# Another issue table for a fused attention and gate kernel: 272 runs of value blocks instead of 356

## The chip, the cores and the metric

The kernel runs on one core of one Trainium2 chip. The metric is the device time of one execution in microseconds (us). Times before come from three runs and from one profiled execution, whose trace gives the start and length of every instruction.

## What is computed

```python
def reference(A_x, A_wqkv, A_wo, B_x, B_w1, B_w3, B_w2):
    x = A_x                                   # [1, 2048, 512]; B_x is not used
    xn = layernorm(x)
    # A: attention, 32 heads of 16
    qkv = (xn @ wqkv).reshape(B, S, 3, 32, 16).transpose(2, 0, 3, 1, 4)
    q, k, v = qkv
    p = softmax(einsum("bhqd,bhkd->bhqk", q, k) * 16 ** -0.5)
    s = einsum("bhqk,bhkd->bhqd", p, v).transpose(0, 2, 1, 3).reshape(B, S, 512) @ wo
    # B: gated feed-forward, 1792 wide, on the same xn
    h = silu(xn @ w1) * (xn @ w3)
    g = silu(h @ w2)
    return x + s * g
```

All of it is float32.

## The kernel before

A prologue (up to about 159 us) normalizes the tokens, makes queries, keys and values, and stores queries and keys in DRAM. A main part then does the attention and the gate together, and a short end finishes the output.

**Products in float32.** Matrix products are done as three products of a high and a low half of each operand (names end in h and l: xth, xtl, wh, wl). In the attention the three stand below each other in one contraction: a head's 16 rows appear as 3 x 16 rows of queries and keys.

**Two row halves.** Scores, maxima and gate products contract over 64 rows or fewer, so TensorE's array is used as two halves of 64 rows, lower and upper, that can run one matmul each at the same time. Value products contract over 128 keys and use the whole array.

**The letters.** The main part's order of matmuls is written out in the string `ORDER_OF_ISSUE`, one letter per piece of work. A small letter stands for the lower half of the array, a capital for the upper one:

- `s`, `S`: a score matmul (line 627, tile e), 128 keys by 512 queries of one head of a pair; ScalarE then takes the exponential into a tile pt (line 630).
- `m`, `M`: a matmul for the row maximum of a later phase (line 389, tile m); VectorE reduces it into mp (line 391). A phase is one pair of heads and half of the queries: 32 phases, 16 key chunks each.
- `f`, `F`: one matmul of the gate (line 858, tile f). A product's lower and upper matmuls add up in one bank; ScalarE takes the bank out, GpSimd (POOL) does the rest and splits weights and hidden rows.
- `v`: a value block (line 640, tile pv): the four exponentials of a chunk times the values, 8 instructions in the trace. It needs the whole array.
- `r`, `R`: the small work that turns a phase's maxima into rows of the query tile, a transpose on TensorE among it; `r` is followed by a value block.
- `o`: a piece of the output projection or of the division by the sums, on the whole array.

There are 7 PSUM banks for s, m, f and o together, and one for pv. A **stretch** below is what stands between two pieces of work on the whole array; a **run** is such pieces in a row.

**The planner.** As the program is built, the letters are read one after the other. The class `Model` is an account of time: `half` books a matmul of one half, `whole` one of the whole array, `work` the engine that empties a bank. `SLOT` (0.232) is the time of a half's matmul, `LOAD` (0.1) its weight load, `TURN` (0.097), `VALUES` (0.858) and `CLEAR` (0.983) belong to value blocks. By this account the planner chooses the bank that comes free first, and places DMAs, small work and gate elements that are due. A letter whose work isn't ready by the account goes to a list `late` and is tried again before each next letter:

```python
    for c in ORDER_OF_ISSUE:
        settle()
        small()
        tend()
        catch_up()
        ...
            what = (c.lower(), int(c.isupper()))
            if what in late or not half_issued(*what):
                late.append(what)
```

Nothing of this runs on the chip; the chip sees fixed queues of instructions with semaphores.

Of the kernel before, what the change touches and what calls it, by code (L numbers as in the profile page):

```python
# [55 lines left out]
    "FMfFffFMsFfmFSfMfFfsMfFFfSfMfSfmFvmSMmmFmFvvvsMfSfFSffMfFFsfMFsfFsMFfFsmFSffFmSFffSrvsMfMfSFffFsFmFf"
    "SFmsFfFfMsFFmFsFmFfSmvmSfSMsMfvmSMmMsvvfMfSSfMfSffMfSfFfMfFsFmFsFsFmFfFsFmFsFfMfFfSmMfSfsMffSsvmSSff"
    "MsMvsSmSmMvvSfMffSfMfSfSfMfMfFfFmFsFfFfFsMfFfSmSfFfFmFsFmFmFsFfFsFfFmSfFmFsFfFfMfMfMsMvsMfMMsvsMSmFm"
    "vSmmFFmmFmFmFvvvmSmFfFFmsFFfmFsFFfsFfMSfFfMfSfMfMfSfFffMsFFfSfMfSfFfMfsFsRvvSmMffSfSfMffSfSmFfFsFmFs"
    "FFfMfFsFfsMFffSMffSfFmSfFsFMfFfSfmFsFsFmFFfmFsFSffFmMvSmsSmMvsFmSmSmFvvmFSmsMsFvsMFmMssFvsMMmsSvsFmS"  # L60
    "FmmSvSmfFmSfSfFFfmSfFmFsFFffSmFsFfFMsfFSfMffFFsmMvsMMmmFmFvvvsMfSfFMfFffSmSfFmFsFfFMfSfMfFfsMfFFssFr"
    "vvSmfFSfFmfSFfmSfFsFMfsFFfmFSffFMsfFFsMffSFfMffMMfsFFfFfMsfFFmFsFfMfmFsFFfMfmFFfMsvvSmsSSmvmSsMvvMff"
    "SSffFMfFssFmFfFsFMfsFFfMfSfmFsFFffFfMSffMSffSfMfFsFfMsFfFmFsFsFmFfFsFmFmFfSmvmSmSSfvmSmMMsvSmSmvSmSf"
    "FfMffFSfmSFfMfsFfFmFsFFfMfsFmFFmFfMfmMvvvMsMsfFfFFsfFMsfFsFFfmFFssFFfMfSffSsFrvvSfMffSfMSffSfMfMfFfS"
    "fFsFmFfFsFmFsFmFsFfFsMfSfFmMvSmmSmFFsvSmmSMsvMsMfsFsFfFFfMsfFFsmFSffFMsFffMfFMfSfMsvmSMmfSvvMfSsfFmF"
    "FfFsmFFfsFMfSffSmFFffSMfFfSfMmvSmFmmFsFvSmmSMsvSmmFfSSffFfFmSfFsFMfFsfFMsfFFsMffSFfMmvSmFmMmvvSfMffM"
    "fSfSfSfMfFfFsFmFsFfFmSfFsMfFfFmFsFmFmMvvrsMFfsFMfFsFfMsFfsFMfSfFfmSfFmFsFmFfFMfMfmSvvSfMfMffSfSfMfSf"
    "FfMfFsMfFsFfMfFsFfMsFsFfFmFsFfMmFfMfSvSmsMMsvSmmSfMvsMMmSffSvvMffSfMfSfMfSfSfFfFmFsFmFsFfSfMfFsFmSFf"
    "FmSfFsFmFfFsMfMfFsMfFsFFsFfFfMfSfMssFvSmMmFsvSmFsmFmSvSmmMsSvSmFsFsmMvSmmFmFsFFmmFmFvvvMsfSMffSfFfFs"
    "MfFFsMffSFffMsFfSMffMFfSfFfSfsMFfFffSSfsSRvvvsMfMMfSffFFffMsFfFFsfMsFfFMfsFmFSfmFFfSffSfFmFmFsFFmFfs"  # L70
    "FmFFfSffMFfsMvvSmSsMmvSmMmfSvvMfmSFmFsfFfFsFmFFfsFsFmFsFFfmFsFFfMsFfsFMfFsFfmMfFSfSfFmvvSmmSfSFfFfFf"
    "mFfSfMfSFffMsFmFfFsFmFMfmFFfMsvvsMfSsFFmFffFMsFfSfmFFsFfsMFfmFfSFfFsmMvSmmSSfvMssSmMvMsSfMfSmvmSMmSs"
    "vvmSfSSfMfFffFSfMffSSfmFFfsFmFFfFsmFsFfMsFmFsRvvSmFfMfSffMFfMfSffFmFmFsFFfFsMfFffFsFFmMmvsMFmsSvMssS"
    "mMvvmFFssFsMFfFfMffSfFMsfFSfMfsFfFmSFffFfSmSvMmsFfFfFfSFmfSfFSmfFfSmFSffFmSfFmFSfmFfFmMvSmMssFvmSsMM"
    "svmSmFsFfSfFFmsFFfmFSfmFfSFmfFMsFfmMvvsMMssMvMsMsfSMfvvMfSffMMfMffSfMfSffFfFsFmFfFsFsFFmFsFffMsFFfMm"
    "RvSmSfSffMfFfFmSfFfSmFsFfFMsfFmFsFMffFsFSfMmvsMMmmFvvSfmFfSSfmFfFSfmFsFFfmSFfFsmFFsFfMmFffMSfvsMfSMs"
    "vvMfSsFfFmFsfFsFmFfFsFsFMffFmFSffFMfmMvvSfMffSfMSffSfMfSfFfFmFsFmFsFfFsFmFfFsMsFfMmFvsMfSfMmSvSmfSsF"
    "FmfFfFsMFffSmFSfFfMsfFmFsFmFfFMfMfMmvvfSMmMmvvsMFmFsFfFsFfmFsFfFsFMfSfMfSffFfMsFsFMfRvMsfMSffSfSfMSf"
    "vMsMfSfSsvmSSfmMvMsSfSfMsvmSfSFfFmFfFsmFFsmFFfsFFmsFFmFfSffMfMSfFffSMfSffFSfmFsFFfmSfFsFMfMffFmMvsMf"
    "MmMvvmMsMFsFsvsMSmSmvsMFsfFSmFffFmFSfmFfSFffMsFFmfFsMFfSffFFmSfFsMfMfFfsFMffFsFfFMfsSvMfSssMMfvsMmMS"  # L80
    "svSmFmmSvSmmFmMmFvvvmSfFsFmFFsfFSmFfsFFmFsfFSmfFmFmFsFFfsFFmFffMSfMfSffMSfRvsMfMfSMfSffMfSfMfSvSmfMs"
    "FsFFfFfMsFfsFmFFsfFmSfFMfmFsFFfsMvSmmSFfFfsFFfmFSfsFmFmFvvvvmSfFFfsSMffFFfFsmFFsfSfMFfFsFmFmfFmSvSmM"
    "mfMSfvSmSfMsvMsMfsFFfFsFfMsFfsFmFfSfFmSfFfSFmfFmFsSvmSSfMfsMvsMmMMmvvvfSMffSfMSffSFfmFsFFfmSfFsFfFMf"
    "SfsFsFmFFfsFrvMsfMfSfFfSFffMfSFmFsMfFfSfmFfFsFmFFfsFmFmMvsMFfsFFmFsFfsFMfSfSfmFFffSmFSffFmFFmMfvSmMs"
    "SfMfvsMMsSsvmFSmSmvvMffSfMfFsMFffSfMFfsFSfmFSfFfmFfFsFFmFffSMfsFfFFmfFSfmFsFfSmFFfmFSfFmfFSfmFmMvvsM"
    "sMsMvsMMfMsvSfMsFmFsFfFfmFFsFmfFSmFfSfMfFfsFMfMfMfFfMmvvvsMSffSfFfFmFsFfFsFmFFsFffSMfFfSfSmFfSfsFrvv"
    "SmfSfFFfSmfFSmFfSffFSmfFSffMsFFfMfsFmFFmFffMsFfFmFFsfFfSmFfSfFFmsFmFfMFsFfmMvmSfSSmvMsMsMsvsMfMMfSsv"
    "sMMsMsvvMffMSfMffSfFsFfFmFsFmFmFSffFmFsFFfmFMffSvsMSsSmvMfMsfFFssFFfmFFsFfsFmFSffSmFfFfSMffMfFSmvmSM"
    "fsMvSmsSFmmFvSmmSMmvvmSSfSfmFfFFfMsfFFsMfsFfFMsfFMffSsFfFMffMfSSffSfMrMsMsvSmmMsSvvSfMffSSffMfMfMfSf"
    "MfsFfFfFFsFmFsFmsFFfMfsFfMfFMsfFFmSfFffMsFmFFfSfmFfFSfmFfFmSvvSmsSmFFmvSmSmMmvvmFsFMfmFsFFfFsFmFfSff"  # L90
    "MFssFfFMfSffMfSfFfSmFfFsFMsFfFsMfFffMFffSfMSmvvsMmMsMvvSfMfSffMfMfSfMfFsFfFsMfFsFfFsMfFmFsFsFfFmFfSf"
    "MmFfSfSfFmFfSfFmFsFmFfSmFfMmvvMsSssFvrvSmfSSfmFfFfFmSFfFsmFFsFfmFsFsFsFmFfFFfmSFfmFsFFfmFSsfFmMvvSmS"
    "sMmvsMMsSfvmSMsSsvmFSfMfFfsMFfFsmFFfSfmFFfSffMfFsFmFfFMmfMvvMffMfSfSfSfFMffFsFFfMsFfFsmFfFFsmSfFFmmF"
    "vsMMmSfvsMsFFfMfFsFfmSFfSfmFFsfFmSFfmFSfSffFMfmFMmvvSsMsmMvvsMfMfSFffSfMSffMfSfMfFsFsFfMFfsFmFsFmFmF"
    "FmFmFsvvsMfFFmsFfFFmMfsFfFfSFfMsFfSfMfFfSfMfFsMRvvsMMffSSffFFfMsFfSfMfsFfFmFsFFmsFFfmFFmfSmSvSmmSSmv"
    "SmMfsSvMssMSmvsMsFFmFfFfSmSfFfMfSfFmSfFfFmSfmFFsmFfFMmvvMsfSMfsMvMsmSsSvMsFmsFsFfFfFmFSffSmFFsFfMfsF"
    "fFMfmFMffSvsMmSsMvsMfMSfSmvsMfMfMsFfFFfSfmFfFSmfFfSfMFfSffMmFmFvvvvRFsFmFfMffFSffMfFfSfFmFFsfFmSFfSf"
    "mFFsfFmFFffSMffMfSfFsFfFmFsFsFmFsFfSfMfFfMsFfFmFmSvmSsFFfMfFsfFMsFfFsfMFsFfsMfFFmSfFmFfSffSMmvSmsSsM"
    "vMssSMfvmSsMsMvSmfFmSFffSFfmFSfMffSfMFfsFmFFfsFmFmFFmvvMmSfMsSfvSmmMsSvSfMsFfsFMfFfsFmFsFFfMsfFfMsFs"
    "FFfMfFfMfSfMfMfSfMfvsMMsMfMfvSsMmvSmfMMmSfvSfmMMmvvvSmsFFffFmFsFFssFmFFfFfSfmFFssFmFFfSfmFfFSfmFsFfF"  # L100
    "MfsFSfRvvSfMffSSffSMfSffMfMvsMMfSsFfFfFfsMFfFsfMsFFfmSfFFsfMfSFfsMFffFmSfFfMsFfFsFmFFsFfmFFfMffSmMvS"
    "mmMfSvSmMmsFmFvvmFSmsSmFvSmSmmSvSfmSfMSffFfFsFMfsFFfMsFfFsMffFSfMffSfSfMfFsFmFsFfFMsfFSfFmmFfFmMvSmM"
    "fMsvSmmMFmvvvmSFmmFFsFfFfsFmFfFsFFmFsFsfFmFFmsFFfSfMfSffFMfSffFmFSsRvvsMsMSmvSmfSSffMFfFfMsFfsFMfFsF"
    "fMsFfFsmFsFFfmMvSmmFmMvvSfMffSfMfSfSfSfMfFfFsFmFsFfFmFsFmFsFfFsMfMfFsSvMsSmsFsFvvmFfSSfSfMffFfSMffFF"
    "mSffFmFsFFmfFsFMfMmvvSmsSMmvsMMmFfSffFfFSmFffFSfmFmFSffFsFmFFmFffMmMvvvmSMffSfSfMffSsFmFFfsFmFFsfFMs"
    "fFsFfMfFFsMfsFSfsrvvSmSfmFfFFfSfmFmFsFFffSFmfSfFmFsFMffFfMfMsMvsMfMfSFffSfFmFsFmFSffFmFsFsFmFsFfFmMv"
    "mSsMSffMvsMmMsSvmSsMfSfMvsMsMSmvSmMfSfsFfFFmsFFmfFsFFmfSFmFfSfFmfSMffFsMvMmSffSsMvsMMfFssFFfFmFsFfmF"
    "sFMfMfSfFffFSfmFMmFfMfMfvSmMmvvvMsfSSfFfmFfFSfFfmSFfSsfFmFFffSfFMfsFsFFsrvMsFsFsFmFffFsMFfSfmFSffFSm"
    "fFFsMfSfFfmMvSmmMmFvvSfMffSfSMffSfSfMfFfFsFmFsFfMfFsFsFmFsFfMfFsFmMvSmmFmSFsvSmSsmSvMsSmFfFfMffFsFmF"
    "FsfFFsMfFfSfMmfFSfMfvMsMsSmvvMffSMffSfSfMfSfFfMsFfFsMfFsFmFsFfFmSfFfMsFfFmSsFfMmvsMsMsMvsMMfMsvSmSfS"  # L110
    "sMfvMfmSfSSmvmSMmMmvvvMfSfMffMSffMfSfFfMfSfFfMfSfFmFsFsFfFmFfSfFmFsFmFfSfSfFsSRvvsMfFsFFmFsFfFmFsFfM"
    "fMffSfFsFfFfFsFmFsFmFsFfFmFsFsFmFFmfFsFFfFmSfFmSmvSmmFmSvvSfMffSfSSfMffMSffMvsMfSMmvvmSfMsFFsfFFfmFF"
    "fsFmFSfFmSfFfmFSffFfSmFsFsFMfFfFsmFSffFMsfFMffSSffFSfMfmMvvsMMssMvSmMmfFSfFfFfsFFfmFsFmFsFfFFsmFFfsF"
    "mFFsmFFfsFFmmFfMfMMfvvvSmfMSffSfMfSffSmFFfsFFmfFFsFmmFsFfFSfFmSfFffMfSRvvSmsFsFFmFffFFmsFFfmSfSFfmFs"
    "FfFmMvsMsMsMvsMMsSfMfvSmMmsSvsSMfSfmMvsMMfMfsFFffFsFMffFsMFfFsFfFmSfmFfSFffFMmvsMMsMsvvMffSfFSfmSfFF"
# [1238 lines left out]
```

## Time and profile before

| | before |
|---|---|
| median of 3 runs | 1740.28 us (1740.03 to 1740.57) |
| span of the profiled execution, first to last instruction | 1737.7 us |
| TensorE busy | 1730.3 us |
| VectorE busy | 1432.1 us |
| ScalarE busy | 1254.2 us |
| GpSimd busy | 765.5 us |
| granted TensorE clock, mean | 1.000 |

The profiled execution's own time is its span and what lies around it; the span is 2.6 us under the median of the runs. In the lines of the profile PE is TensorE's matmuls, PEld its weight loads, DVE VectorE, ACT ScalarE, POOL GpSimd. A line of the timeline has the start and the length in us, the engine, the line of the kernel, the operation, the tiles written and read, the shapes, and how many instructions were merged. A trace does not say which half of the array a matmul is on; that follows from the table's letters.

### The profile page before, as it was taken

Reading aid. Unit: us, or ns where it says so; the run is one execution under the profiler, and the core shown is the slowest. Engines: PE = TensorE matmul, PEld = TensorE weight load, DVE = VectorE, ACT = ScalarE, POOL = GpSimd, SP = SyncE. Lnnn points to the kernel's source line nnn. Section 1 sums busy time; section 2 is a strip of 40 time slices with the busy share of each in tenths; the row PEclk is TensorE's granted clock in tenths of the full one; section 3 lists DMA queues with packets and bytes.
Section 4 is the critical chain, followed back from the end, with each engine's and each line's share of the span. In section 5 each row is a group of like instructions: output and inputs, shape, how many; then the busy total and the mean of one; then the engine's idle time right before and its main releaser. Section 6 shows DMA issues by size and latency. Waiting matters only on the chain.

```text
span 1737.7 us, 35616 instructions
## 1 busy us (share of the span) xinstructions
PE 1730.3 (100%) x13236; PEld 1044.5 (60%) x13236; DVE 1432.1 (82%) x2349; ACT 1254.2 (72%) x2440; POOL 765.5 (44%) x793
## 2 busy tenths in 40 slices
...
GB/s 288 241 205 206 65 33 68 50 69 63 80 84 91 53 72 28 69 66 75 105 74 68 57 63 52 46 72 56 135 56 68 70 35 55 115 76 37 180 152 97
DMA packets 147373, 155.36 MB, mean 89 GB/s; under 512 B 42368, under 2 KB 101760, under 8 KB 144224
## 3 DMA queue, kind: packets, MB, share of 16 engines
...
q10 hardware_dynamic: 864, 1.05, 0.2%
...
## 4 chain that ended last, share of the span: by engine, by line
PE 98%; DMA 1%; DVE 1%; SPq 0%; ACT 0%; issue 0%; POOL 0%; POOLq 0%; ACTq 0%
PE f L858 28%; PE pv L640 27%; PE e L627 17%; PE m L389 14%; PE m L507 3%; PE e L195 2%; PE e L199 2%; PE e L197 2%; PE o L195 1%; PE o L199 1%; PE o L197 1%; PE m L480 0%; PE m L404 0%; DMA wl<-g 0%; DMA ovl<-o 0%; PE o L1089 0%
## 5 line engine op out<-in xcount | busy, mean ns | idle before, releaser
L391 DVE TENSOR_REDUCE mp<-m 128x1 f32<-128x512 f32 x2048 | 1298.5, 684 | 164.2 <-PE m L389 89.8
L630 ACT ACTIVATE pt<-e 128x512 f32<-128x512 f32 x2048 | 1085.7, 606 | 268.4 <-PE e L627 121.2
L627 PE MATMUL e<-qs,ks 64*128 64x512 f32 x2048 | 716.0, 411 | 0.0
L389 PE MATMUL m<-ks,qs 62*128 62x512 f32 x2048 | 697.8, 413 | 0.0
L640 PE MATMUL pv<-pt,vt 128*17 128x512 f32 x4096 | 508.7, 596 | 0.0
L627 PEld LDWEIGHTS e<-qs,ks 64*128 64x128 f32 x2048 | 344.6, 185 | 228.7 <-ACT pt L630 85.0
L389 PEld LDWEIGHTS m<-ks,qs 62*128 62x128 f32 x2048 | 334.7, 184 | 141.0 <-ACT pt L630 42.8
L640 PEld LDWEIGHTS pv<-pt,vt 128*17 128x17 f32 x4096 | 84.0, 96 | 206.7 <-issue 199.9
L858 PE MATMUL f<-xth,wh 64*128 64x512 f32 x488 | 171.1, 392 | 0.0
L858 PE MATMUL f<-xth,wl 64*128 64x512 f32 x488 | 170.8, 396 | 0.0
L858 PE MATMUL f<-xtl,wh 64*128 64x512 f32 x488 | 169.7, 392 | 0.0
L743 POOL TENSOR_TENSOR h<-g,h 128x512 f32<-128x512 f32 x56 | 72.0, 1286 | 198.8 <-ACT h L739 198.8
L858 PE MATMUL f<-wh,hs 64*128 64x512 f32 x496 | 157.3, 394 | 0.0
L858 PE MATMUL f<-xth,xel 64*128 64x512 f32 x408 | 146.7, 394 | 0.0
L858 PE MATMUL f<-xth,xeh 64*128 64x512 f32 x408 | 143.1, 393 | 0.0
L858 PE MATMUL f<-xtl,xeh 64*128 64x512 f32 x408 | 142.5, 392 | 0.0
L858 PE MATMUL f<-xeh,hs 64*128 64x512 f32 x400 | 122.7, 393 | 0.0
L322 POOL TENSOR_TENSOR wl<-wr,wh 128x512 fp32r<-128x512 f32 x92 | 118.5, 1288 | 7.7
L322 POOL TENSOR_TENSOR xel<-wr,xeh 128x512 fp32r<-128x512 f32 x76 | 98.0, 1289 | 6.3
L727 POOL TENSOR_SCALAR th<-th 128x512 f32<-128x512 f32 x56 | 34.7, 620 | 143.2 <-ACT th L720 143.0
L321 POOL TENSOR_SCALAR wh<-wr 128x512 fp32r<-128x512 f32 x92 | 57.2, 621 | 86.5 <-PE f L858 85.5
L321 POOL TENSOR_SCALAR xeh<-wr 128x512 fp32r<-128x512 f32 x76 | 47.3, 622 | 101.0 <-PE f L858 48.2
...
## 6 DMA issues: line engine op xcount, KB each, us to landing
...
```

The lines of the kernel that those rows point to most:

```text
L195: nc.tensor.matmul(ps, lhs[1], rhs[0], start=first, stop=False)
L197: nc.tensor.matmul(ps, lhs[0], rhs[1], start=False, stop=False)
L199: nc.tensor.matmul(ps, lhs[0], rhs[0], start=False, stop=last)
L321: nc.gpsimd.tensor_scalar(hi, t, 1.0, 1.0, op0=ALU.mult, op1=ALU.mult)
L322: nc.gpsimd.tensor_sub(lo, t, raw(hi))
L389: nc.tensor.matmul(ps, qs[p % 2][64 * h:64 * h + KM, q0:q0 + P], ks[p % 2][64 * h:64 * h + KM, c * 512:(c + 1) * 512], start=True, stop=True)
L391: nc.vector.reduce_max(mp[p, half][:, h, qt, c:c + 1], ps, axis=AX.X)
L627: nc.tensor.matmul(ps, ks[p % 2][64 * h:64 * h + KR, k * P:(k + 1) * P], qs[p % 2][64 * h:64 * h + KR, q0:q0 + 512], start=True, stop=True)
L630: nc.scalar.activation(pt, ps, AF.Exp, scale=DH ** -0.5)
L640: nc.tensor.matmul(pv[32 * j:32 * j + VW, :], vt[2 * p // GH][:, key, 2 * p % GH + j % 2, :], pt, start=key < 2 if last else k == 0, stop= ...
L743: nc.gpsimd.tensor_mul(h2, g, h2)
L858: nc.tensor.matmul(ps, left[r], right[r], start=starts and lane == 0, stop=ends and lane == 1)
```

## The change

The string `ORDER_OF_ISSUE` is replaced by another one (8611 letters become 8599, since small work that stood as `R` before a `v` now stands as `r`), and the account's `half` changes in two places: a matmul now holds the queue until its half's previous matmul has begun, and it reports the later of the two halves' last starts, as if matmuls of both halves were reported in order. Everything else stays.

```diff
 ORDER_OF_ISSUE = (
-    "MffSfMfSfMfSfSfMfSfMfMfSfMfsMsFFfFffFsMMfMfsFFfFfMsfFfFMsfFmFmFvmMmMFsFffFfFfMFsfFFfFffMSfMffFFmFmfS"
-    "vFmfSFmFfmFfFSfFmFmfFfSfFFmFsFfFfMfMffMMsvSfMfsFfFmFsFMffMsFfFfMsFfFsFMfFsfFMfFfMmvSmmSmFFmvSmmSFmvS"
...
+    "MffSfMfSfMfFFSMffSMfFfSffSfMffMfMMfsffFsFSffmFFsFmFsFmFFfMfMFfMmvvmSSfmFsfFmsFfFMFfsMfFsfSfFMFfMfsfF"
+    "fSfmFfFfMFSfFFSFFfmsfMSffFmFsFmFsFmFfSffFMfmFmFMmFvvMssMfFsFFfmFFsMfsFfFmFFsFmfSMffFfMfMffMfMsMvvmSfS"
...
 )
...
         def half(self, h, there):
 
             load = max(self.issue, there, self.begun[h], self.clear)
-            self.issue = max(self.issue, there)
+            self.issue = max(self.issue, there, self.begun[h])
             begins = max(load + self.LOAD, self.lane[h])
             self.begun[h], self.lane[h] = begins, begins + self.SLOT
             self.turned = False
-            return begins
+            return max(self.begun)
```

More of the change, by code (lines that the diff above doesn't have):

```diff
@@ L56 @@
[L56 to L115, printed above, removed]
@@ L116 @@
-    "mfFSfSfmFmFfFSffFFsmFfFFmsMvSmmSsFfFFfFfMsfFsFMffSFfMsFfmFsFfFFfMfMmMmvvvSsSfmSvMsSfsFFfmFfFfFFsMsFf"
-    "SmfFFfSfMfsFfFMfSfFsRvvSmsSSmvmSsFsFmFfFFfMsFfmFsFmFfFsFFmmMvvSmfSSffSMfvMfSfSffSMmvsMSfSfMfFfFfMsfF"
-    "sFMfsFFfMsFfSfmFSffFMmvSmFmFsFffFfMSffFMfSfmFSfSffFmFSfFfmFsFsFmFmFFmmFvvvMfSfSfmFfSfFfMsFFfMsfFSffM"
-    "sFFfMsFfFmFmmFvSmmFSsvsMSsmMvsMfFFsmFFsfFMsfFsFMfFsfFMfSfSfMffMfFmFMfmMvvvSmsMsSvrsMfSfFfMfSfFMfsFFs"
-    "MfsFfFMfsFfFSmfFsFmFFffMfMfSfMffSfSFfFmFmsFFfsFsFmFFfFsFmFffMmMvmSsFSmvSmmSSmvSmMsmFFsvsMMffSSffFFmf"
@@ L121 @@
-    "SFmFsFmfFfSSfFmfFfSMffSFmMvsMMssMvsMMsMfMfvvMfMfSfMffSfMfSvsMfMmFSfFfFfSmFffFSfmFmFsFFfmFsFfFsFmFSfF"
-    "fmFsFmFmFSfFffFMfMmMfvvvMsSssSvrvSfMffMfSMffSfMfSfMffSfFfFsFmFfMsFFfmFFsfFFsFmfMfSmFFfsFFfFsMffSfMSf"
-    "FfmFsFmFfFSmvsMMssFmFvsMmMsSvsMmFsFFfSfFfmFsFmFsFfFmFsFMffFSfFmFmSfFfsFFmMfFfFfMfMsvSmMfSfsMvsMSmSmv"
-    "SmSfmSSfvMsfMSmfSvvmSfMfMSsvSfmMsFsFFfFfsFmFsFfFmFsFsFmFsFfFFsmFFfSfsFMffFfFMsfMFfMmvvmSmSMmvvvmSfSf"
-    "SFffMfFSfSfmFFffSmFfSfFmFFssFFmFfFsrvSmfMSfFffSfFmSFfsFmFsFFfMsFfmFSffFmFSmfFSsvMsSmfMvsMfSfSmFFffFm"
@@ L136 @@
-    "vorSsSsovSsSsSsSovsSSssSosSSsSsvvSsSssSvvoSsSsSsvovSssSsosSsSovSsSsovsSovsSSsoSvvvoooooSssSSsoSsoosS"
-    "sSosSSsvvvv"
+    "MffSfMfSfMfFFSMffSMfFfSffSfMffMfMMfsffFsFSffmFFsFmFsFmFFfMfMFfMmvvmSSfmFsfFmsFfFMFfsMfFsfSfFMFfMfsfF"
+    "fSfMfFfFMfSFfSFFfmsfMSffFmFsFmFsFmFfSffFMfmFmFMmFvvMssMfFsFFfmFFsMfsFfFmFFsFmfSMffFfMfMffMfMsMvvmSfS"
+    "fMfFfSFfmSFfFsFmFfFmSmfFSfFfFfmFmMfFMmvvsMFMsFffsFfFsMFfsFfMMfFfMsFfFsfFfFmFMfMfMmvvmSfMFsFfSfFmfSFf"
+    "SffMFsFmfSFfmFSfFmFfFmFsMmvrvSfMfSfFMffFSfSfFmsmFFsSfmFfFfSFmffSFmSFffFmfFMfSfSfFfMsfFmFsFmFSfmFfFsF"
@@ new lines @@
+    "FmSffFmFMmfFMmFvvvFsMmMmmvvSmsFfFMfsFfFMsfFfMSfFfMfsFMfFsfFfFMfSffMSffSfFFMFfsmFsfFmFFsFmFsfFmSFfMff"
+    "MmFfmMvvvmMMssSvMsFmsFFsmFFfsFFfMffSfMFsMffFSfmFfSMfFfsFfMMsvmSSmSmvrSmmSMsvvsMfFmSsFfFfMFsfFfMsFMfs"
+    "FFmFfsFFmfFSffMMsvSmSfMfffSfMfSfMffSFfMsFsFfMfsFFmsFFfMsfFmFSffFfFFmSmmMvvvSmmSsMvSmsSfMMfvmSMmsSvmS"
+    "MfSffFSFFffMSfMfSfffMssFmsfFFmfSfFMFsFfmFFsmFFfsFmFsFFsfmFFfSmSfFfMfFMfMfffMfMMmvvvsMSmsMvMsSfMfFffS"
+    "fMSffMfSFfSfMfsFfFmFsFfSMfFfsFmFFsfMFffSFmfSFfmFsFmFsFmFFfmFmFmSvvMmmSSmvrSmsFFmFsFmFfsFFfSmfFsFmFFs"
@@ new lines @@
+    "FfmSFfmFSfFffSMfSfFmSffFfMfSmFFsfMFfFfMfSfMMffMmMvvvmMMssvmSFmFsFmsFFfsFfFSmFfsFFmfFsFFmmFSffFfSFmSf"
+    "FmfFSfFfMmFmfFmMvvSmFMsmFsvMmMsMsvvsMMsSmvMsmFsFFmFsFsFffFMsFffMSffMfFSfFffMfMfSmMFvrSmfmSFsfFmFFsfM"
+    "SffFFmfSFsfMfFfSMfSffFmFFffMfSfFfSMfFsmFsFfMFfsFFmsFFfsMFfMffFFmsmMvvvsMMmSsvvMsfMSfSfFffMSffMSfFffM"
+    "sFFmfSFfsFmfFsFFmFsFfmFFfSMFfsfFMsfFFsFmFfSfMsfFmFsFMfmFfFMfmMvvvvsSmfmSFFfFmFsfFMfSFfmSfFSffSmFFfSm"
+    "ffFFmSmfFmFSFvsSSMsssvvvsMmSsvrSmFmFsmFsFFfsFFffMSfFsMfFfMfSffMfFFfSfFMMsvsMssMmvmSSfMfSfFffMSfFfsMf"
@@ new lines @@
+    "FfSfMfSFfmFsfFmFFsmFfFSFfSmfFFfSmFffSmFfSfFFmSFfmSffFsFmFmFMmvvmMMssSvvvvmSFsFmfFsFfFsMfFsFFmFsFfMsf"
+    "FfMFfSfSffMMfmSvvMssMFsFMvMfSfMfSfSffFMfsmsFfmFsFFmFfSFmfSfFffMFFmmMmvvMsfSfMfSFffMSffFmSfFfSmsFfFFm"
+    "SfFFmsFsFfFFsFssSvvvMFsmssFFfFmFsFmfFfSMfsFfMFfSfMfSfFfSffSFsMFmvvvMsfsSMffFfMFffSMffSfMfSFfSfFmFsfF"
+    "mSfFfMsFFfFmsFMfmSvsMSsmSvrMsMmmSvvFMffSMffSffMSFffSfMsfFmsFfSFmFsfFmSffFMsfFFmSfFFsmsFFfMFfsfMfSFmF"
+    "sfFFmSfMffFsSFfmMvvsMMsmSvmMmFFmMmvvvsMFsMfFfsFFmsFfFMsFfFsMffFfSMfSfFmSfFffMSfMfFsFsfFFmfSFfMfSffFF"
@@ new lines @@
+    "fSsFmsSvvsMsMMsvsMMfSfFffSfMfSfFSfFmsFfMFsFfFmSfFmFfsMfFfFSffMSfmFfSFfFsmFSfFfFmmFmFFmFmvrvvvmSFmFsF"
+    "fsFFfmSfFfSFmfFsFFmFsFfSmFfSfmFsFfFmSFfFssFFsfFsMvvfSfMfSFfMfSfMfsFSfmFFfsFFmsFfFmSFffFFfmSFmmMvvSmS"
+    "mmSvmMsFmSsFvSmmMSsvsMSffSMfFffMSffFFmsFFmfSmFfFsFFmfFMffMMFmvvSmmSfFfFsFmFsFffSFmFsfMSffFfMSfFfmFmM"
+    "FfsMFvvsMsMMsvsMfMmSFvrmSsmFfsFfFMsFfFsMfFsFfMsFfMffSmFFfffSMfFFSffMSffMfSfmsfFsFMsfFfFMsFFfsMfmFmFf"
+    "FFmSmvvSmMmSsvvvMsSfMffFfSfMfFmSfFFsFmsFfFmFsFFmsFMfFfSffMMmvvSFmfMfFsFfSfFmfSFmsFFfFmSfmFSffFFsSffF"
@@ new lines @@
+    "SfFsSvvvsMfMsSffFfMmFfSFfSfmFSfFfmSFfsFmFffSmFffFFMfSFfsMfFsFmfFFsFmFFsmFSffsFMffFFfMsfSMsvvvMsMsSsv"
+    "vrSmSfMfFfFsfMSfFfsMfFFmsFFmFfsFFfmSFfSffMfFFfMFFfSfSfmsfMFfsmFFsFmFsfFFmSffMfFfSsFSsvvvvSmMsSmvsMFf"
+    "MsfSfFfMSffSfMfsFFmFsfFFMsfFsFMffFfsFFfMfMfSFfsfFMFsFfmsFfSmFfSfFFmFffFmSFmFmMvvmMsFmSmFvvSmmMsSvsMf"
+    "MSfSffFfMsFfMSffFFsFmsFFfmSFffMsFfFSfMfSfSmvvvSssMMsvvsMMFfSfffSfMfSFfMSfffMSffSfMsffFSffMFsfFMsFFsf"
+    "MFfFsfMsFfmFFsFmFfSfMFfsmFFsFfMfFFmFmmMFvrvmSsFmfFfSFmsFFmFffSMffSMfFfSfsFMffSfFMfFsFmFsFfFsFmFsmFfS"
@@ new lines @@
+    "fFFmFffMMfMffMMmvvvMmmSmSvvSmFffMSfFffSMfsFFmfFSffMFsMfFsFmFffSmFFsFfSfMfsFFmfSFfmFfSFmFsFFmfSfFfSmM"
+    "vsSsMSmvvSsMsSsvvSmmFfSFffSFmsFfFSmfFFsmFsFFfMfsFfMFsFsFfMfFsFmfFFfMssFSFmFmsvMmSmvrSmMsSmvSmFmFssFf"
+    "FfFSmFfSffMFsfFsMfFFmFsfMFfMfSfmMvvsMmMmSvvsMSmMsvfMSfMfSFffSfMffSmSfFfMsFfFmFsFMffFsFmFsFFfmfFSfFsM"
+    "fFfFmSFfFsFmsFFfMsfFmsFfFmFfMSmvvmSSSfMfvvmSmSMsvvSmSmSmvmSmFsFFsfFfMmFfSfFsFmFffSfMSFfMfsFffSffMFFf"
+    "MfSfMfSfFsFFmsfFMsfFFmFsfFfMSffFmFsFmFMmvvMmMmMmvvvsMSmfFfFFfSfFmsFFfMfMfSfFfsFfMFsfMFffsFfFMSfFfMff"
@@ new lines @@
+    "SfMsfFmFSfFsFmfFsFFmfFSsmFFfMmFrvmSMmsSvmSmSFfsFFfmsFFfFmSFfFsfMSfFfMsfFFffMmFfSSmvMsmMsMFvvfMSfMFFf"
+    "fSffSmsMffsFFmFFsFmsfFFmSffMfFfFMssMvvsMmSMmvvSmFmFssFmFFsFfFfmSFffSfMSffFmSfFfFmFMfSfsMvvSmSmSmvvSf"
+    "MfSfFfMSfffMsfSFmFfFsFmSFfmFFsmFFsMfFfmFfFMmSvrMsmfSfSfFfMsFfMFfsFfMsfFMfFsFFsmfSFfffMFfFMfSfFfMSfSf"
+    "mfFFFsmsFFfMsfFFsMfFFsFfsFmMsvvsMMssMvSmFfSfMffSfFsMFfSfMfSfFfmFsFmFFsFmFfsFfMFffMFfMfMfMmMvvvmSMfmm"
+    "MvvfSMffSfSfMffMSfSffMsFfFmSfFFsmFFsfFmsFFfMFsffSmFFsFFmSfFfmSFfmFsFFmfFfMFfMSmvrvvMssMMsvMsMfSfSFff"
@@ new lines @@
+    "fMSffMfSfsmFsfFMSfFfmFsFfSfMFfsFFmfSfFMsfFsFmFfsFFmSfFFmsfFMfFSmfFMmvvvmMSmSmvvSmFsFmsFFfFmfSfFSmfFf"
+    "SMfSfFfMfsFFmSffFFmSfmFSffSFffMsFfFmSfFmFSSfFmFfSfFsmvvMsFsmFsMvMsMssMvmFFmMmMmvvvMsmFFsfFsFFmsFfFSm"
+    "fFFsmFFsFffMfSmFSffFmFSffSFfSsFfsSvvSmmSSmvmSFsmFsFsFFmfFfFMsFfMfSfFffMSffMsFFmFffMFfMFMsvrmSmsFsFsm"
+    "FfFfMfFsFMffMsFFffSMfSffMfSfFfFMfFFSffSfMfSfmffSFmsFmFsFFfFmmFsFmFmFvvvsSSsMsvvmMsMfSSfvMmSsmSvvsMfF"
+    "MfsFfMFfMsfFFsfFsFfMfSfFFmSfFfMsfFfFMffSfMfSfMfSfFFsmFFsFfmFsFFmsFFmFfmSFfmSvvmSSmsMvmfFMsMMvvmSmsFS"
@@ new lines @@
+    "fFfFmfSFsFmfFfSfMSffFSmFfFmSffFfffSMFMfFfSfMffSFsmFFsfFmFFsfFmSfFFffFFmsMmMvvSsmMsMvrMsmSmMvvMssFFms"
+    "FmFFsfFFfMsfFMffSfMFfSfMfFsfFFfMFffSfMfSfFfMFSfsmfFsmFFFsMfFsffMSfFsFfmFFmMmvvSmsSMmvsMMffSfSfFfMmFf"
+    "SfFSfFmsFfFmFsFFmsFmFFfMfMfsSvsMSmsMvsMFfsfMfSFfFMffSMfsFfFmFSfFmFsfmFFfmFFfMSmvvvMmSsMmvvmSsFfMfFFs"
+    "mFSffFMsFfSfmFSfFfmSFfMfmFFmfFMmFvvfSMffMfSMffSfsFFsFmfFFsMfsFFfMsFfMfmFFfFssMvvsmSSFmfFFfFmsFFfSmfF"
+    "fSfMFsfFMsFfFmsFfMffSfMfSSvvMmSmMsvrSFmSffMfSFfSSfMfSffMSvvmMfsffSFmsFFfMsFfFsfMsFfFMfFsFmFfmSFffSFs"
@@ new lines @@
+    "FmFfFsfMFsFfMsfFMfSfFfMfFMffSMsvFmSsmmSvMmsMmSvvmSmMsMvvsMsFFmsFfFFmfSFfSmfFSfmFfFfSMfSffSFmFffSFmfS"
+    "FfMfFsFmSffFmFSfMfmFfMFfMmFvvmSmFSsfFfFmsFFfSmfFFsFmsFfFMfSfMfFsfMFfSfmFFsFsfFMsfFFfMsfFMfFffMMffMMf"
+    "SmvvrSmmMMsvvMsMsSmvmSsFFmFfFsFmfFmSsFFfmFFsfFsMfFfSFmSfFfmSFfFmsFFmfFsFsFmMvsSsSsMvvSsSsMfSfvvMsSsv"
+    "MsfSMffFmSffMFfSFfSfMfsFFfmFsFmFsFFfSfFmFmmMFvvvMsfSmFsfFfMsfFMfSfFfMsFsFfMSfFfmFffSFmFFffMFfSfFFsmf"
+    "fFSFmFsffMSfFFmsFFsFsffSFSsvvvfSfMMffSfFMFsffSFsmFFfSfFmSffFSmFfFsmFfFFmFSFmvrvSmmsFffSFmsFFfSmFfsFm"
```

45 lines of the change are left out of this document (32 added, 13 removed).

## The prediction

> **What bounds the kernel now.** I read the page first (busy shares, the chain that ended last), then the groups and the waits, then the timeline of TensorE around single changes between value blocks and half-array matmuls.
>
> ```profile
> span 1737.7 us, 35616 instructions
> PE 1730.3 (100%) x13236; PEld 1044.5 (60%) x13236; DVE 1432.1 (82%) x2349; ACT 1254.2 (72%) x2440; POOL 765.5 (44%) x793
> ...
> PE 98%; DMA 1%; DVE 1%; SPq 0%; ACT 0%; issue 0%; POOL 0%; POOLq 0%; ACTq 0%
> ...
> L391 DVE TENSOR_REDUCE mp<-m 128x1 f32<-128x512 f32 x2048 | 1298.5, 684 | 164.2 <-PE m L389 89.8
> L630 ACT ACTIVATE pt<-e 128x512 f32<-128x512 f32 x2048 | 1085.7, 606 | 268.4 <-PE e L627 121.2
> ...
> L640 PE MATMUL pv<-pt,vt 128*17 128x512 f32 x4096 | 508.7, 596 | 0.0
> ```
>
> TensorE never rests and is 98% of the chain. VectorE pays 1298.5/2048 = 0.634 us per maximum and ScalarE 1085.7/2048 = 0.530 us per exponential, and both have air:
>
> ```profile
> 159.40:1621.70 1462.30, 1462.30 (x11817) 857.39 (x11816) 1274.51 (x2074) 1147.05 (x2223) 722.84 (x737) 1.00 0.27 69
> 1621.70:1717.70 96.00, 94.30 (x571) 49.50 (x567) 40.79 (x65) 60.49 (x121) 4.33 (x5) 1.00 0.46 146
> ```
>
> These are windows (TensorE, weight loads, VectorE, ScalarE, GpSimd, clock, DMA). In the first, from the first gate matmul to the last, TensorE is busy all the time, VectorE 87%, ScalarE 78%, and the clock is full throughout. So the order of TensorE's work alone sets this time: what the table of letters wastes is the cost. I compared the trace with the table of before: split at the value blocks, every one of its stretches has exactly the letters that the table gives it. The table is what runs.
>
> **Prices.** A value block uses the whole array, the letters s, m, f (either case) half of it. The timeline shows single changes:
>
> ```profile
> 812.12 1.05 PE L640 MATMUL pv<-pt,vt 128*17 128x512 f32 x8
> 813.11 0.50 PE L389 MATMUL m<-ks,qs 62*128 62x512 f32 x1
> ...
> 813.45 0.40 PE L389 MATMUL m<-ks,qs 62*128 62x512 f32 x1
> ...
> 813.69 0.39 PE L389 MATMUL m<-ks,qs 62*128 62x512 f32 x1
> 814.01 1.05 PE L640 MATMUL pv<-pt,vt 128*17 128x512 f32 x8
> 815.00 0.49 PE L627 MATMUL e<-qs,ks 64*128 64x512 f32 x1
> ...
> 815.81 0.39 PE L389 MATMUL m<-ks,qs 62*128 62x512 f32 x1
> 816.13 1.05 PE L640 MATMUL pv<-pt,vt 128*17 128x512 f32 x8
> ...
> 700.50 3.63 PE L640 MATMUL pv<-pt,vt 128*17 128x512 f32 x32
> 704.06 0.49 PE L389 MATMUL m<-ks,qs 62*128 62x512 f32 x1
> ```
>
> A lone value block takes 813.11 - 812.12 = 0.99; four in a row take 704.06 - 700.50 = 3.56, so a further one costs (3.56 - 0.99)/3 = 0.857 and a run has about 0.13 of its own. The stretch of six letters (three slots, both halves at work in each) takes 814.01 - 813.11 = 0.90; that of eight (four slots) 816.13 - 815.00 = 1.13. A slot is 0.23, and the stretch has 0.90 - 3 x 0.23 = 0.21 beside its slots. Measured in the same way over all 356 stretches of before (the two above are among them), the line through them is 0.197 + 0.235 per slot, with a scatter of 0.06, and 213 lone value blocks take 0.983 on average, 0.125 over 0.858. I use these: **0.322 for each run**, 0.235 for a slot. The fit leaves little for real stalls: before is nearly as good as its order allows.
>
> A half without a partner pays the full slot:
>
> ```profile
> 1621.11 0.50 PE L627 MATMUL e<-qs,ks 64*128 64x512 f32 x1
> 1621.12 0.72 PE L389 MATMUL m<-ks,qs 62*128 62x512 f32 x2
> 1621.45 0.39 PE L627 MATMUL e<-qs,ks 64*128 64x512 f32 x1
> 1621.68 0.39 PE L858 MATMUL f<-wh,hs 64*128 64x512 f32 x1
> 1621.69 0.39 PE L389 MATMUL m<-ks,qs 62*128 62x512 f32 x1
> 1621.91 0.39 PE L627 MATMUL e<-qs,ks 64*128 64x512 f32 x1
> 1622.24 1.48 PE L640 MATMUL pv<-pt,vt 128*17 128x512 f32 x12
> ```
>
> Seven letters take 1622.24 - 1621.11 = 1.13, as long as the eight above.
>
> **The change part by part.** The numbers of letters are the same in both tables (4032 gate halves, 2048 scores, 1984 maxima, 512 value blocks, 22 projections), and so are the copies, splits and DMAs that hang on them; they move with the letters, on queues that the windows show with room (GpSimd 722.84 of 1462.30, DMA 0.27). Free unless a letter waits for one of them; that price is in the second rival. The two edits of the account give the chip nothing by themselves: they change the planner's times, so which bank it picks and when small work is put in. I take nothing for it; what it costs if it goes wrong is in the last rival.
>
> *Fewer runs.* Counted alike (everything between stretches of half matmuls, projections too), the table goes from 356 runs to 282; value runs alone from 349 to 272. 74 fewer at 0.322: **-23.8 us**.
>
> *Unequal halves.* The longer half of each stretch, summed, goes from 4053 to 4111 slots (32 stretches of odd length become 90). 58 x 0.235 = **+13.6 us**.
>
> *Halves out of step.* Before is issued pair by pair: of 356 stretches, 343 never have one half more than one letter ahead; nowhere are there three letters of one half in a row. The new table has 157 such runs of three or four, in 71 stretches. What does that cost? The queue of weight loads is worked in order, which one wait shows (TensorE, then its loads):
>
> ```profile
> 228.87 0.39 PE L858 MATMUL f<-xth,xel 64*128 64x512 f32 x1
> ...
> 229.07 0.18 PEld L389 LDWEIGHTS m<-ks,qs 62*128 62x128 f32 x1 [0.18 <-ACT pt L630]
> 229.07 0.18 PEld L858 LDWEIGHTS f<-xtl,xeh 64*128 64x128 f32 x1
> ```
>
> The gate's half had begun its matmul at 228.87 and could have loaded the next weights then; it loads at 229.07, right behind a maximum of the other half that waited for a bank. In running order a load comes when its half's last matmul begins, and after a value block the matmul of 813.11 lasts 0.50 instead of 0.40: a load that nothing hides costs 0.10. So in fFFSMf of the new first stretch, with the first f and F both at 0, the next F, S and M begin at 0.23, 0.46 and 0.69. M's load goes at 0.46, the load of the f behind it no sooner, and that f begins at 0.56 instead of 0.23: 0.33 late, and its half stays late unless the other gives it time back. I went through both tables letter by letter with just these three statements (0.23 a slot, loads in table order and not before the half's last matmul begins, 0.10 from load to matmul): the old order loses nothing in any stretch, the new one in 56 stretches **+11.1 us**.
>
> Starts are not held in table order. At this place the table has F, then m; yet the m began first:
>
> ```profile
> 1602.46 0.39 PE L389 MATMUL m<-ks,qs 62*128 62x512 f32 x1
> 1602.62 0.39 PE L858 MATMUL f<-wh,hs 64*128 64x512 f32 x1
> ```
>
> m overtakes F by 0.16, because its half was ahead. [...]
>
> *A last stage without gate matmuls.* The new table has its last f or F earlier: behind it, up to its last maximum, stand 108 scores, 87 maxima and 29 value blocks in 30 stretches (before: 38, 13, 11). TensorE needs 29 x 0.858 + 30 x 0.322 + 107 slots x 0.235 = 59.7 us there; ScalarE 108 x 0.530 = 57.2 and VectorE 87 x 0.634 = 55.2. That is 96% and 92% of TensorE's time, against 78% and 87% above, with nothing to put in when a bank is late. From below nothing; from above what a single bank wait takes, at most 0.9 a time:
>
> ```profile
> PEld e L627 <- ACT pt L630: 85.0, 112, 0.9
> ```
>
> (the wait of a weight load, mostly hidden under value blocks). If a third of the 30 stretches wait 0.9, that is 9. I take **+2.5 us**, nearer to nothing because TensorE still has the largest need.
>
> **The sum.** -23.8 + 13.6 + 11.1 + 2.5 = +3.4. The profiled span is 1737.7 and the median of the runs 1740.28, so 2.6 lie outside the span; I leave them. Span 1741.1, time **1743.7 us**. A measurement of this kernel can tell about 0.2% (3.5 us) from no change; the forecast lies at the edge of that.
>
> **The rivals.**
>
> *Halves that hold each other up less (faster).* If a load passes a load of the other half that is not yet due, or if the loss of the order falls where a bank or an exponential would have been waited for anyway, the +11.1 goes and the last stage costs nothing: 1740.3 - 23.8 + 13.6 = 1730. For it: the 0.16 overtaking of starts. Against: the load at 229.07. Half of that would be 1736. Chance 0.18.
>
> *Banks become the bound (slower).* Runs of two value blocks and more rise from 126 to 164 (of three and more from 33 to 62), and stretches grow from 22.7 to 28.6 letters on average. In a run of three (0.99 + 2 x 0.857 = 2.7 us) VectorE can work off 4 maxima and ScalarE 5 scores, nine banks where there are seven; so both run dry and have to make it up in the stretches. VectorE's air is 1462 - 1275 = 187 us. From the point where a stretch has more maxima than VectorE takes at 0.634 plus what the banks hold, TensorE waits. 38 more such runs x 0.3 us (a third of the longest wait of 0.9) = 11, with the other terms 1740.3 + 0.9 + 11 = 1752. For it: 87% already; against: the windows show no wait of TensorE at 87%. Chance 0.24.
>
> *Starts in table order.* The same walk with each matmul starting no earlier than the one before it loses 34.8 instead of 11.1: 1743.7 + 23.7 = 1767. The 0.16 above speaks against it. Chance 0.04.
>
> *The table is not what runs.* A letter whose bank or input the planner does not see in time is put off to a later place. Before had none that crossed a value block; if 1 in 100 of the 8064 did, 80 halves alone at 0.235 make up to 19 us: 1740.3 + 0.9 + 19 = 1760. Chance 0.05.
>
> **How the numbers follow.** The forecast's own case (1738 to 1749) has 0.49. Within 0.2% (1736.8 to 1743.8) lies most of its lower half and a little of the first rival: 0.37. Faster by more: 0.18, the first rival with its half-way forms. Slower by more: 0.45, the upper part of the forecast and the other rivals. The range that holds 8 in 10 leaves out the far end of the first rival and the last two: 1732 to 1757.
>
> **What would show it.** Right: TensorE still at 100% and 98% of the chain; a lone value block 0.99, a stretch of seven letters as long as one of eight; about 282 runs; long stretches with three letters of a half in a row 0.2 to 0.5 longer than their slots. The time of stretches beside their slots should fall by 74 x 0.197 = 14.6 and rise again by the 11.1. Wrong: waits of weight loads for ScalarE and VectorE (lines 627 and 389) well above today's in the part with gate matmuls; a span under 1734 would mean that the halves do not hold each other up, one over 1750 that banks decide.

## The result and the profile after

| | before | after |
|---|---|---|
| median of 8 runs each | 1740.33 us (1739.78 to 1741.32) | 1745.56 us (1744.77 to 1748.04) |
| after to before | | 1.0034 (95% interval 1.0024 to 1.0044) |
| span of the profiled execution | 1737.7 us | 1745.4 us |
| TensorE busy | 1730.3 us | 1718.7 us |
| span less TensorE busy | 7.4 us | 26.7 us |

The new table is slower by 5.2 us or 0.3%. The forecast was 1743.7 (1732 to 1757). The profiled execution of after took 1747.16, 1.6 above the median, so the 7.7 us between the two spans are a little more than the medians differ by.

The page of after, the same lines that were shown of before (line numbers of after are one lower than before's, since its table has one line less):

```profile
span 1745.4 us, 35654 instructions
PE 1718.7 (98%) x13236; PEld 1093.0 (63%) x13236; DVE 1419.9 (81%) x2349; ACT 1241.0 (71%) x2440; POOL 765.4 (44%) x793
...
PE 94%; DVE 4%; ACT 1%; POOL 0%; DMA 0%; issue 0%; SPq 0%; DVEq 0%; POOLq 0%; ACTq 0%
...
L390 DVE TENSOR_REDUCE mp<-m 128x1 f32<-128x512 f32 x2048 | 1288.2, 685 | 214.3 <-PE m L388 141.6
L629 ACT ACTIVATE pt<-e 128x512 f32<-128x512 f32 x2048 | 1073.1, 606 | 285.3 <-PE e L626 157.2
...
L639 PE MATMUL pv<-pt,vt 128*17 128x512 f32 x4096 | 498.2, 596 | 0.0
```

The same 13236 matmuls take TensorE 11.6 us less, and it rests 19.3 us more: -11.6 + 19.3 = the 7.7 of the spans. So the table did save array time, more than the forecast gave it, and lost it again to waits that the forecast had not seen. In the chain VectorE and ScalarE have 5% where they had 1%.

The windows of after, in the same columns as before's (TensorE, weight loads, VectorE, ScalarE, GpSimd, clock, DMA), the main part cut at 1600:

```profile
159.40:1600.00 1440.60, 1424.80 (x11641) 893.09 (x11639) 1228.64 (x2017) 1112.06 (x2182) 714.39 (x729) 1.00 0.28 70
1600.00:1725.00 125.00, 119.80 (x747) 61.79 (x745) 73.04 (x121) 82.28 (x163) 12.62 (x13) 0.97 0.34 112
```

In the first stretch before had no idle time of TensorE at all; now there are 15.8 us. In the second there are 5.2, and the granted clock is no longer full.

Which instruction the idle time stands in front of is seen in the groups: the last column is the idle time of TensorE ahead of the group and what ended it. This is the transpose of the small work in before,

```profile
L404 PE MATMUL m<-ident,nm 128*16 128x128 f32 x32 | 8.9, 277 | 1.7 <-ACT nm L400 1.7
```

and in after:

```profile
L403 PE MATMUL m<-ident,nm 128*16 128x128 f32 x32 | 9.0, 280 | 19.3 <-ACT nm L399 19.1
```

Of the 19.3 us that TensorE rests more, 17.6 are in front of 32 transposes, and they wait for nm, the negated row maxima that ScalarE writes. Nearly all that is left is one wait of a gate matmul for hidden rows (hs) that GpSimd has to split first:

```profile
L857 PE MATMUL f<-xeh,hs 64*128 64x512 f32 x400 | 127.6, 392 | 1.8 <-POOL hs L744 1.8
```

The timelines of one place with a transpose, first TensorE, then VectorE, then ScalarE (start, length; in brackets the idle time before and what ended it):

```profile
1230.39 1.05 PE L639 MATMUL pv<-pt,vt 128*17 128x512 f32 x8
1232.45 0.28 PE L403 MATMUL m<-ident,nm 128*16 128x128 f32 x1 [1.01 <-ACT nm L399]
1232.66 1.91 PE L639 MATMUL pv<-pt,vt 128*17 128x512 f32 x16
```

```profile
1230.01 1.89 DVE L390 TENSOR_REDUCE mp<-m 128x1 f32<-128x512 f32 x3 [0.26 <-PE f L857]
1231.93 0.22 DVE L396 TENSOR_REDUCE mx<-mp 128x16 f32<-128x64 f32 x1
```

```profile
1232.18 0.22 ACT L399 ACTIVATE nm<-mx 128x16 f32<-128x16 f32 x1 [0.64 <-DVE mx L396]
```

The phase's last maxima keep VectorE to 1231.90; only then it can reduce mp to mx, ScalarE negates mx, and TensorE, which had ended its value block at 1231.44, transposes. What stands behind the transpose in TensorE's queue begins after it, the next value block at 1232.66. Of the 32 transposes, 20 start within 0.15 us of the end of nm in after, and one did in before, where half of them start 4.9 us or more after it.

The banks are not the cause. Waits of weight loads in after from 160 us to the end of the main part (us in total, times, longest); before had 85.0 for the first:

```profile
PEld e L626 <- ACT pt L629: 45.9, 62, 0.9
PEld m L388 <- DVE mp L390: 44.1, 63, 1.3
PEld m L403 <- ACT nm L399: 37.9, 21, 4.1
```

The wait for exponentials fell by 39.1, and the new third line is the transposes'. That of maxima for their reduction rose; in before it was

```profile
PEld m L389 <- DVE mp L391: 30.4, 52, 0.9
```

The four lines in which a score or a maximum waits for ScalarE or VectorE are 220.1 us together in before and 158.6 in after.

### The profile page after: what moved, and what is told of

It is laid out like the page before. It is cut to its first block, busy times and chain, and to the rows that moved or that the text cites. A ratio compares the mean times of both kernels' runs of the same rounds, so it can differ in the third digit from the quotient of the medians.

```text
span 1745.4 us, 35654 instructions
## 1 busy us (share of the span) xinstructions
PE 1718.7 (98%) x13236; PEld 1093.0 (63%) x13236; DVE 1419.9 (81%) x2349; ACT 1241.0 (71%) x2440; POOL 765.4 (44%) x793
## 4 chain that ended last, share of the span: by engine, by line
PE 94%; DVE 4%; ACT 1%; POOL 0%; DMA 0%; issue 0%; SPq 0%; DVEq 0%; POOLq 0%; ACTq 0%
PE f L857 27%; PE pv L639 26%; PE e L626 15%; PE m L388 15%; DVE mp L390 3%; PE m L506 3%; PE e L194 2%; PE e L198 2%; PE e L196 2%; PE o L194 1%; PE o L198 1%; PE o L196 1%; PE m L403 0%; PE m L479 0%; DMA wr<-in_A_wqkv_dram 0%
## 5 line engine op out<-in xcount | busy, mean ns | idle before, releaser
L629 ACT ACTIVATE pt<-e 128x512 f32<-128x512 f32 x2048 | 1073.1, 606 | 285.3 <-PE e L626 157.2
L388 PE MATMUL m<-ks,qs 62*128 62x512 f32 x2048 | 706.2, 415 | 0.0
L639 PE MATMUL pv<-pt,vt 128*17 128x512 f32 x4096 | 498.2, 596 | 0.0
L626 PEld LDWEIGHTS e<-qs,ks 64*128 64x128 f32 x2048 | 344.5, 185 | 140.6 <-ACT pt L629 45.9
L639 PEld LDWEIGHTS pv<-pt,vt 128*17 128x17 f32 x4096 | 90.4, 96 | 221.8 <-issue 213.0
L857 PE MATMUL f<-xth,wh 64*128 64x512 f32 x488 | 175.0, 393 | 0.0
L857 PE MATMUL f<-wh,hs 64*128 64x512 f32 x496 | 153.4, 393 | 0.0
L857 PE MATMUL f<-xtl,xeh 64*128 64x512 f32 x408 | 148.1, 392 | 0.0
L857 PE MATMUL f<-xeh,hs 64*128 64x512 f32 x400 | 127.6, 392 | 1.8 <-POOL hs L744 1.8
L857 PEld LDWEIGHTS f<-xth,wh 64*128 64x128 f32 x488 | 86.3, 185 | 8.5 <-issue 4.3
```

The source lines that it names most:

```text
L388: nc.tensor.matmul(ps, qs[p % 2][64 * h:64 * h + KM, q0:q0 + P], ks[p % 2][64 * h:64 * h + KM, c * 512:(c + 1) * 512], start=True, stop=True)
L626: nc.tensor.matmul(ps, ks[p % 2][64 * h:64 * h + KR, k * P:(k + 1) * P], qs[p % 2][64 * h:64 * h + KR, q0:q0 + 512], start=True, stop=True)
L629: nc.scalar.activation(pt, ps, AF.Exp, scale=DH ** -0.5)
L639: nc.tensor.matmul(pv[32 * j:32 * j + VW, :], vt[2 * p // GH][:, key, 2 * p % GH + j % 2, :], pt, start=key < 2 if last else k == 0, stop= ...
L857: nc.tensor.matmul(ps, left[r], right[r], start=starts and lane == 0, stop=ends and lane == 1)
```

## The experiments

The theory after the result (A): a letter `r` or `R` forces the reduction, the negation and the transpose of a phase to be issued one behind the other; the new table puts it where the phase's last maxima have just been issued, and TensorE waits for the two other engines. The rival (B): the waits replace bank waits that would come at the same places anyhow, so moving the letter gains nothing. A second question is which part of the change does it, and a third whether the prices of the forecast hold.

**The small work of eight phases, one run later.** In after's table, `r` goes to the last value block of the next run; all other letters stay. One of the eight places:

```diff
-...MMsvmSSmSmvrSmmSMsvvsMfF...
+...MMsvmSSmSmvvSmmSMsvrsMfF...
```

> The new table, with the small work of 8 of the 31 phases (2, 5, 11, 14, 15, 16, 20, 21) put one run of value blocks later, so that the transpose of the row maxima stands further behind the reduction and the negation that it needs. Theory A (TensorE stands still at these transposes): in the trace of the new kernel these eight runs are 8.8 us longer than a run with a transpose that does not wait, so the time falls from 1745.6 to about 1737 (1735 to 1740). Rival B (the loss sits in the halves that are out of step and in bank waits; the transposes only take over a wait that TensorE would have anyway): no change, 1744 to 1748.

Measured: 1739.16 us (1737.25 to 1741.95), 0.9995 of before (0.9986 to 1.0005). The group of transposes:

```profile
L403 PE MATMUL m<-ident,nm 128*16 128x128 f32 x32 | 9.0, 280 | 11.4 <-ACT nm L399 10.8 <-ACT pt L629 0.5
```

7.9 us of idle time are gone from here, and the time is 6.4 under after. The last phase's wait of 3.2 us remains, with several smaller ones.

**Six more phases, to the end of their own run.** Beside the eight, six such edits; one of them:

```diff
-...FfFFMmSvrMsmfSf...
+...FfFFMmSvvRMsmfSf...
```

> As before it, and in six more phases (13, 22, 24, 26, 27, 30) the transpose goes to the end of its run, behind the last value block. Theory A: another 0.5 to 0.9 us each, 5 in all: about 1732 (1730 to 1736), faster than both kernels. Rival B: 1744 to 1748.

Measured: 1732.98 us (1732.21 to 1733.50), 0.9958 of before (0.9941 to 0.9974). With not one score, maximum or gate matmul moved, the table is 12.6 us faster than after and beats before. (The lines of this kernel are numbered as before's.)

```profile
L404 PE MATMUL m<-ident,nm 128*16 128x128 f32 x32 | 8.9, 277 | 6.5 <-ACT nm L400 5.9 <-ACT pt L630 0.5
```

Idle time before the transposes fell by 12.8 from after's 19.3, the time by 12.6. B is out.

**The last phase's small work behind a piece of the projection.** Half of what is left in the row above is one wait, of the last phase. The `o` that followed it is put ahead of it, on top of the two edits above:

```diff
-...SMmvMmMmMmMvRosSsSS...
+...SMmvMmMmMmMvoRsSsSS...
```

> The kernel with 14 transposes put later (1733.0), and the last phase's transpose put behind the first piece of output projection (2.9 us on TensorE) instead of ahead of it. In its trace TensorE stands still for 3.2 us at this transpose, and its clock is at half for 3.4 us after. Theory A: most of the 3.2 goes and with it the slow clock, 3 to 5 us less: 1728 to 1730. If the projection waits for something that lands as late, or the scores of the last phase come later by as much: 1732 to 1734.

Measured: 1729.27 us (1728.57 to 1729.80), 0.9934 of before (0.9919 to 0.9949). It is the fastest of all, 11.4 us under the before of its own runs and 16.3 under after. From its page:

```profile
span 1728.0 us, 35652 instructions
PE 1716.3 (99%) x13236; PEld 1092.4 (63%) x13236; DVE 1420.5 (82%) x2349; ACT 1240.1 (72%) x2440; POOL 764.2 (44%) x793
```

```profile
L404 PE MATMUL m<-ident,nm 128*16 128x128 f32 x32 | 8.9, 277 | 3.5 <-ACT nm L400 1.9 <-DMA inl<-g 1.0 <-ACT pt L630 0.5
```

**The account alone.** Before's table with the new `half`:

```diff
-            self.issue = max(self.issue, there)
+            self.issue = max(self.issue, there, self.begun[h])
...
-            return begins
+            return max(self.begun)
```

> The old table with the changed account alone. Theory A and B alike: the order stays pair by pair, so the account has nothing to say: 1739 to 1742. If the account by itself moves banks and small work to worse places: above 1744.

Measured: 1739.67 us (1739.37 to 1740.22), 0.9995 of before (0.9986 to 1.0004). Nothing.

**The table alone.** After's table with the old `half` (the same two lines the other way).

> The new table with the old account. With the account of before the planner issues it in the same runs and stretches as with the new one (280 stretches, 4066 slots), and negation and transpose together in the same 20 phases. Theory A: the table carries the whole change, 1743 to 1748. If the account matters for banks or small work: outside of that.

Measured: 1747.67 us (1746.40 to 1749.19), 1.0040 of before (1.0025 to 1.0055), with as much idle time in front of the transposes as in after. The table carries the whole change.

```profile
L403 PE MATMUL m<-ident,nm 128*16 128x128 f32 x32 | 9.0, 280 | 19.2 <-ACT nm L399 19.1
```

**Small work early, in before.** If the position of the small work is the cause, before must lose by it too. Whenever a phase's reduction has been issued, its negation and transpose follow at once, ahead of the next value block:

```diff
         if c in "rv":
...
+            if rows and rows[0][2] < 2 and not rows[0][2] == 0:
+                second()
             issue_v()
```

> The kernel before, with one thing taken over from the new one: as soon as the reduction of a phase's maxima has been issued, the next value letter issues the negation and the transpose too, in all 31 phases. Order of halves, runs and slots stay. Theory A: each transpose then waits about 1 us more, as in the 20 phases of the new kernel where negation and transpose are issued together: 25 to 33 us, so 1765 to 1774, with TensorE's loads waiting for the negation. Rival B: hidden under value blocks, 1740 to 1744.

Measured: 1839.79 us (1836.97 to 1842.57), 1.0571 of before (1.0555 to 1.0587). The direction is A's, the size three to four times what I expected. Page, transposes and core of this run:

```profile
span 1838.5 us, 35619 instructions
PE 1759.6 (96%) x13236; PEld 1048.4 (57%) x13236; DVE 1432.1 (78%) x2349; ACT 1259.0 (68%) x2440; POOL 763.7 (42%) x793
```

```profile
L404 PE MATMUL m<-ident,nm 128*16 128x128 f32 x32 | 9.5, 297 | 73.1 <-ACT nm L400 73.1
```

```profile
core 0: 1838.5 us, clock 0.983
```

The span grew by 100.8: 71.5 of them are idle time, nearly all in front of transposes (73.1 against 1.7), 31 waits of 0.8 to 3.2 us, about 2.4 each. The other 29.3 are busy time, though the work is the same: the granted clock was at half for 61.4 us after such waits, and by an estimate 61.4 at half clock lose half of that, 30.7.

**Halves out of step.** In before, 114 times in long stretches, three pairs of letters are regrouped so that three of the lower half come first and then three of the upper; the numbers and the runs stay. The first of the places:

```diff
-...MMFsFffFfFfMFsfFFf...
+...MMFsFffffFFMFsfFFf...
```

> The kernel before, with three pairs of letters in the middle of each of 114 long stretches put out of step: three matmuls of the lower half, then three of the upper one, in place of three pairs. No run and no slot is added. If weight loads go in table order and no sooner than their half's last matmul begins (the rule of the prediction, 0.33 a place): 37.9 us more, 1775 to 1781. If matmuls also start in table order: 52.9 more, 1790 to 1796. If the halves don't hold each other up: 1740 to 1742.

Measured: 1766.75 us (1766.42 to 1768.50), 1.0151 of before (1.0136 to 1.0166): 26.1 us over the before of its runs, 26.1/114 = 0.23 a place.

```profile
span 1765.0 us, 35614 instructions
PE 1757.7 (100%) x13236; PEld 1073.8 (61%) x13236; DVE 1434.7 (81%) x2349; ACT 1260.9 (71%) x2440; POOL 765.5 (43%) x793
```

TensorE's busy time grew by 27.4 and its idle time not at all: no wait shows. The 114 stretches with such a place are 0.23 longer on average than their slots cost, the other 242 less than 0.01. That is as much as one slot; that one half runs alone for it is an estimate. None of the three rules that had been written down (0.33 a place, 0.46, nothing) gives that; the one of the forecast is nearest. It is too high by 0.10, as much as its term for a load that nothing hides; that this is the reason is not shown.

**Thirty runs more.** In before, in 30 runs of two value blocks, the first is put ahead of the last pair of letters of the stretch in front, which makes one run more each. The first of them:

```diff
-...FfMfMFmvvSfmMM...
+...FfMfMvFmvSfmMM...
```

> The kernel before, with 30 runs of two value blocks after a long stretch split in two: the first block goes ahead of the stretch's last pair. 386 runs instead of 356, the same slots. At 0.322 a run: 9.7 more, 1749 to 1751. If what a run costs lies beside other work: 1740 to 1743.

Measured: 1750.76 us (1750.14 to 1751.03), 1.0056 of before (1.0039 to 1.0073): 10.1 us, 0.34 a run. The price of 0.322 holds.

## Why the prediction was right, and for which wrong reasons

The forecast said a few us slower, and it is 5.2. That is luck: two errors of nearly the same size cancel. Its sum had +0.9 for TensorE's order and +2.5 for waits; the profile has -15 for the order (busy time -11.6, with 3.4 in it that a half clock takes, see the last section) and +19.3 of waits.

**Fewer runs, -23.8: right.** I listed the letters as the program issues them: 280 stretches instead of 356, so 76 fewer, and at 0.322 that is -24.5. The thirty runs more give 0.34 as the price. (The title sets 272 runs of value blocks beside 356 runs of every kind; counted alike, the tables have 272 and 349 of value blocks, or 282 and 356 of every kind.)

**Unequal halves, +13.6: about +3.1. Halves out of step, +11.1: about +1.7.** Both were counted on the table's letters, on the statement that the table is what runs. For before that is exact. The new table isn't issued letter by letter: 190 letters are not ready by the account when their turn comes (most of them f and F) and go in later, and this evens the halves out. What is issued has 4066 slots (13 more than before, not 58), 50 stretches of odd length (not 90), and the forecast's way through the letters, one by one (the walk), finds 1.7 us of lost time in it. I had the possibility as a rival, with the wrong sign: I priced letters put off as halves left alone, and here they mend the pairs. The price of a place out of step, had there been as many, was too high as well: 0.23 measured, 0.33 forecast. Stretches with three letters of a half in a row were to be 0.2 to 0.5 longer than their slots; 44 of the stretches issued have such a place, and they are 0.04 longer on average.

With these the order's sum is -24.5 + 3.1 + 1.7 = -19.7; the profile shows -15. Most of the 5 us between them lies at the transposes again: the 30 runs that hold a transpose and no `o` take, without the idle time that the profile shows and with half clock counted as half, 0.36 us each over 0.858 a block and 0.125 a run; in before they take 0.23, which makes 4.0 us. Why a transpose takes longer there, no run shows.

**A last stage without gate matmuls, +2.5: the size of the waits was too small, and they are not the banks'.** The last gate matmul of after starts at 1585.27. Behind it the stretches take no more than 0.5 us in total over what their slots cost at the clock that was granted. But TensorE rests at two transposes, 2.00 us at 1607.45 and 3.20 at 1651.75, and both times the clock falls after it. The timeline of the second, the last phase's:

```profile
1650.70 1.05 PE L639 MATMUL pv<-pt,vt 128*17 128x512 f32 x8
1654.95 0.38 PE L403 MATMUL m<-ident,nm 128*16 128x128 f32 x1 [3.20 <-ACT nm L399]
1655.05 0.76 PE L194 MATMUL o<-ks,xtl 128*128 128x512 f32 x1
1655.61 0.63 PE L196 MATMUL o<-xeh,xth 128*128 128x512 f32 x1
...
1658.32 0.39 PE L198 MATMUL o<-ks,xth 128*128 128x512 f32 x1
```

VectorE had ten maxima of the last phase to work off before it could make mx, as its timeline shows:

```profile
1648.03 6.37 DVE L390 TENSOR_REDUCE mp<-m 128x1 f32<-128x512 f32 x10 [0.26 <-PE m L388]
1654.43 0.22 DVE L396 TENSOR_REDUCE mx<-mp 128x16 f32<-128x64 f32 x1
```

Moving one `o` ahead of this transpose gave 3.7 us (1732.98 to 1729.27).

**The step that failed: small work moves with the letters and is free.** The forecast took it as "free unless a letter waits for one of them" and looked for waits at the banks of scores and maxima only. Of the diff it was noted only that some `R` had become `r`. What it should have asked of each `r` and `R` is how long before it the phase's last maximum stands; the chain behind that maximum (the maxima still queued on VectorE, 0.22 for mx, 0.22 for nm) is in the rows of before. What the runs show in place of nothing is 17.6 us of idle time in front of the transposes, and 1.8 in front of a gate matmul that waits for its split; putting 15 letters elsewhere took 16.3 us off the time. Of its signs for "right", TensorE at 100% and 98% of the chain failed (98% and 94%), and so did the 11.1 us of halves out of step (the walk finds 1.7 in what is issued); the number of runs (280 for 282) was nearly as it said.

**Banks become the bound:** not so. The longest line of bank waits fell from 85.0 to 45.9, although VectorE now works through longer runs. **Starts in table order:** at 114 places that rule expects 0.46 each; 0.23 were measured, half of that, and in after matmuls begin up to 0.56 us ahead of one that was issued before them (at 1582.88).
